# A chunked recurrence followed by an MLP on one Trainium2 core: preparing each chunk on 120 full rows with products in column tiles, one masking eviction, no early weights, and another scheduling mode

## The chip, the core and the metric

The kernel runs on one NeuronCore of a Trainium2 chip. Its engines are TensorE (PE, whose weight loads stand apart as PEld), VectorE (DVE), ScalarE (ACT), GpSimd (POOL) and SyncE (SP); DMAs are issued from queues of SP and POOL. The metric is the device time of one execution in microseconds (us), and smaller is better.

## What is computed

For 32 heads (4 batches x 8) a state of 40x40 is carried over 768 steps. Each step reads the state and then changes it; afterwards all heads of a token, 320 numbers, go through two dense layers.

```python
for t in range(S):
    y[:, :, t] = np.einsum('bhd,bhde->bhe', rt, state)
    Sa = np.einsum('bhde,bhe->bhd', state, at)
    state_decay = state * wt[:, :, None, :] - np.einsum('bhd,bhe->bhde', Sa, bt)
    state = state_decay + np.einsum('bhd,bhe->bhde', vt, kt)
...
h = x @ w_in
sp = np.where(h > 20.0, h, np.log1p(np.exp(np.minimum(h, 20.0))))
g = h * np.tanh(sp)
return (g @ w_out).astype(np.float32)
```

`x` is 3072 x 320, `w_in` 320 x 2048, `w_out` 2048 x 320. All inputs are 64-bit; the recurrence's inputs are turned to 32-bit on the host, and the weights are turned to 32-bit pairs (a high and a low part) on the chip.

## The kernel before

The 768 steps are cut into 12 chunks of 64, each taken with matrix products. Four kinds of work make up a chunk, and chunks are taken in pairs.

**Preparation** (`pre_a`, L126 to L203), twice per chunk, once for each half `be` of the heads. It loads the decays and `a` (tile `wa`) and `b`, `k` (tile `bk`) into rows 0 to 39 and 64 to 103, two heads groups `al` of 40 rows, so 80 of 128 rows carry data. On DVE it forms running products of the decays with two scans (L147, L157), scales `a` (L152) and `b`, `k` (L170). ACT copies the scaled `a` into a block layout `ad` (L155), one half on rows 0 to 63 and the other below, so that one PE product per slot (L186, 128 rows by 128 columns by 168 moving columns) gives all inner products of the two heads in that slot; the zeros of the layout keep the heads apart. There are 8 slots per call, and three groups of up to three slots are taken out of PSUM: two scaled copies into `GP` (L188, L189) and one copy into `HA` (L190) on ACT, a masked product into `HA` (L191) on DVE, and one more mask over `GP` (L193). PE transposes `bk` (L202), ACT takes that out (L203). The products of the decays, `P`, go to memory from POOL's queue (L172) for the second part of the kernel. The tiles `wa`, `bk`, `ad` and `P` have two buffers each; the tiles in PSUM named `pa` have two here.

**Inverse** (`pre_inv`, L205 to L221) once per pair of chunks: one transposition on DVE (L209), 60 small DVE operations one after another (L214, L216), and two transpositions (L218, L220). `post_inv` (L223 to L260) makes of it the tiles `KT` with PE products (L232, L241, L258) and ACT copies.

**Step** (`step_a` to `step_c`, L273 to L346) once per chunk, in two halves `g` of the heads: it carries the state from chunk to chunk: products L284, L293, L304, L314, L334, L339 on PE, evictions on ACT, masks (L316) and the state's update (L342, L346) on DVE. Its inputs are loaded from POOL's queue (L267, L270, L271), and `yD` is stored from it (L370).

**MLP** (L482 to L612): weights arrive in pieces (`split`, L488; `load_f32`, L446): a DMA into `cv_d` (L453), then one ACT operation (L459), three on DVE (L461 to L463), one on ACT (L494) and one on DVE (L495). One buffer serves all pieces. 12 pieces make `w_in`, 8 make `w_out`. `early` (three pieces of `w_in`) has its own memory from the start; `first` (the other nine) uses the memory that the preparation's pools leave, so it follows the last preparation; `second` starts `w_out`. Then `load_x` reads `yD` and `pD` back, and per block of 512 tokens PE makes 8 rounds of the first product (L584) and the second (L604 to L606).

The order on each engine is set by the tile framework's scheduler, from priorities: the tables `OFF`, `SORD` and `ORDER` move pieces of the program up or down. The first four chunks are prepared ahead of the first step; each later pair is prepared two pairs ahead.

Of the kernel before, what the change touches and what calls it, by code (L numbers as in the profile page):

```python
# [7 lines left out]
F32 = mybir.dt.float32  # L8
# [5 lines left out]
C = 64  # L14

NHA = 8
NBKN = 8
NA = 2
NWA = 2
# [5 lines left out]
NGP = 2  # L25
# [5 lines left out]
NAD = 2  # L31
NTMP = 1
NP = 2
# [14 lines left out]
def layouts(inp, S=768):  # L48
# [30 lines left out]
def attention(ctx, tc, I, yD, pD, nch, M):  # L79
# [28 lines left out]
    for w, b in zip(wab, bkb):  # L108
        V.memset(w, 1.0)
        G.memset(b, 0.0)  # L110
    for t in [d1] + [x.rearrange("p s k a t -> p (s k a t)") for x in adb[:NAD]]:
        A.copy(t, z.broadcast_to(t.shape))
# [10 lines left out]
    RW, W2, HA, BKN, GP, KT = {}, {}, {}, {}, {}, {}  # L123
    LQ, SQ, OQ, PQ = (dict(S=SP, G=G, A=A)[x] for x in QS)

    def pre_a(c, be):  # L126
        n = 2 * c + be
        wa, bk, ad = wab[n % NWA], bkb[n % NWA], adb[n % 2]
        for al in range(2):
            q = slice(al * 64, al * 64 + 40)  # L130
            LQ.dma_start(out=wa[q], in_=I['wa'][c, be, al])
        for al in range(2):
            q = slice(al * 64, al * 64 + 40)
            LQ.dma_start(out=bk[q, :, 0:128], in_=I['bk'][c, be, al])
        if (c, be) == (0, 0):
            LQ.dma_start(out=cst, in_=I['cst'])
            for t in bkb:
                A.copy(t[:, :, 128:168], cst[:, 256:296].unsqueeze(1).broadcast_to([128, 8, 40]))
        wz, a = wa[:, 0:521], wa[:, 528:1040]
        P = pw.tile([128, 520], F32, name="P", bufs=NP)  # L140
        E = wa[:, 520:1040]
        w2 = pw.tile([128, 2, 8], F32, name="w2", bufs=4)
        wz3 = wz[:, 0:520].rearrange("p (s j) -> p s j", j=65)

        V.tensor_reduce(out=w2[:, 0], in_=wz3[:, :, 1:33], axis=AX.X, op=ALU.mult)
        V.reciprocal(d1[:, 64:584:65], w2[:, 0])
        V.tensor_tensor_scan(out=P, data0=wz[:, 0:520], data1=d1[:, 64:584], initial=0.0, op0=ALU.mult, op1=ALU.add)  # L147
        P3 = P.rearrange("p (s j) -> p s j", j=65)
        E3 = E.rearrange("p (s j) -> p s j", j=65)
        V.tensor_copy(w2[:, 1], P[:, 64:520:65])  # L150
        a3 = a.rearrange("p (s t) -> p s t", t=64)
        V.tensor_tensor(out=a3, in0=a3, in1=P3[:, :, 0:64], op=ALU.mult)  # L152
        for al in range(2):
            q = slice(al * 64, al * 64 + 64)
            A.copy(ad[q, :, :, al], a[q].rearrange("p (s k t) -> p s k t", k=2, t=32))  # L155
        V.reciprocal(d1[:, 64:584:65], w2[:, 1])
        V.tensor_tensor_scan(out=E[:, 0:519][:, ::-1], data0=wz[:, 2:521][:, ::-1], data1=d1[:, 1:520][:, ::-1],  # L157
                             initial=0.0, op0=ALU.mult, op1=ALU.add)
        W2[be] = w2
        if be == 1:  # L160

            RW[c] = wk.tile([128, 2, 16], F32, name="rw", bufs=4)
            pt = ps_g.tile([128, 2, 16], F32, name="pa")
            for b2 in range(2):
                for al in range(2):
                    PE.matmul(pt[b2 * 64:b2 * 64 + 64, al], ident[:, al * 64:al * 64 + 64], W2[b2].rearrange("p a b -> p (a b)"),
                              start=(al == 0), stop=True, skip_group_check=True)
            A.copy(RW[c], pt)
        bk4 = bk[:, :, 0:128].rearrange("p s (x t) -> p s x t", x=2)
        V.tensor_tensor(out=bk4, in0=bk4, in1=E3[:, :, 0:64].unsqueeze(2).broadcast_to([128, 8, 2, 64]), op=ALU.mult)  # L170
        for al in range(2):
            PQ.dma_start(out=pD[c, be, :, al], in_=P[al * 64:al * 64 + 40])  # L172

        if c % 2 == 0 and be == 0:
            GP[c // 2] = iw.tile([128, 32, 2, 32], F32, name="GP", bufs=NGP)
        gp = GP[c // 2]
        u0 = (c % 2) * 16 + be * 8
        ha = iw.tile([128, 8, 104], F32, name="HA", bufs=NHA)
        HA[c, be] = ha
        oa, oh = (0, 40) if be == 0 else (64, 0)  # L180
        og, ok = (0, 64) if be == 0 else (64, 0)
        for s0 in (0, 3, 6):
            m = min(3, 8 - s0)
            pt = ps_g.tile([128, 3, 168], F32, name="pa")
            for j in range(m):
                PE.matmul(pt[:, j], ad[:, s0 + j].rearrange("p k a t -> p (k a t)"), bk[:, s0 + j], start=(j == 0), stop=True,  # L186
                          skip_group_check=True)
            A.mul(gp[0:64, u0 + s0:u0 + s0 + m, 1], pt[0:64, 0:m, og:og + 32], -1.0)  # L188
            A.mul(gp[64:128, u0 + s0:u0 + s0 + m].rearrange("p u k i -> p u (k i)"), pt[64:128, 0:m, og:og + 64], -1.0)  # L189
            A.copy(ha[:, s0:s0 + m, oa:oa + 40], pt[:, 0:m, 128:168])  # L190
            V.tensor_tensor(out=ha[:, s0:s0 + m, oh:oh + 64], in0=pt[:, 0:m, ok:ok + 64],  # L191
                            in1=maskH.unsqueeze(1).broadcast_to([128, m, 64]), op=ALU.mult)
        V.tensor_tensor(out=gp[:, u0:u0 + 8, 1], in0=gp[:, u0:u0 + 8, 1], in1=maskG.unsqueeze(1).broadcast_to([128, 8, 32]),  # L193
                        op=ALU.mult)

        bkn = wk.tile([128, 664], F32, name="bkn", bufs=NBKN)
        BKN[c, be] = bkn
        G.memset(bkn[:, 640:664], 0.0)
        for s0 in (0, 4):
            pt = ps_g.tile([128, 4, 2, 64], F32, name="pa")  # L200
            for j in range(4):
                PE.transpose(pt[:, j].rearrange("p a b -> p (a b)"), bk[:, s0 + j, 0:128], ident)  # L202
            A.copy(bkn[:, s0 * 80:s0 * 80 + 320].rearrange("p (s a e) -> p s a e", a=2, e=40), pt[:, :, :, 0:40])  # L203
# [61 lines left out]
    def step_loads(c):  # L265
        for be in range(2):
            SQ.dma_start(out=VS[be][vrow[be], :, 0:320], in_=I['vN'][c, be].rearrange("i (g s) d -> i g (s d)", g=2))  # L267
# [391 lines left out]
```

## Time and profile before

| what | us |
|---|---|
| three timed runs | 823.36, 827.55, 829.61 (median 827.55) |
| span of the profiled execution | 821.8 |
| PE busy | 722.7 (88% of the span) |
| DVE busy | 458.7 (56%) |
| ACT busy | 428.7 (52%) |
| first inverse ends on DVE (end of L220) | 100.5 |
| sixth inverse starts on DVE (L209) | 368.3 |
| first product of the MLP on PE (L584) | 460.7 |

The times are of whole executions; the span runs from the first to the last instruction of one profiled execution, and no time of its own is given beside it, so it is read against the runs: it is 1.6 under the fastest of them and 5.8 under their median. Four stages are told apart by the events of the last three rows: the start, the steady part, the transition and the MLP.

### The profile page before, as it was taken

The page shows a single profiled execution, that of the slowest core. Times are in us where ns is not written, and L with a number is a line of the kernel's source. Part 1 is how long each engine was busy: PE and PEld are TensorE (multiplying, and loading weights), DVE is VectorE, ACT ScalarE, POOL GpSimd, SP SyncE. Part 2 cuts the span into 40 slices and gives each one's busy share as a digit, 9 for nine tenths or more (in the row PEclk, how much of TensorE's full clock was granted, in tenths as well). Part 3 has the DMA queues.
Part 4 walks back from the last instruction along what each step waited for, and adds up shares of the span by engine and source line. Part 5 has one row for each costly group of instructions (what it writes and reads, how often), then busy time and mean ns, then how long its engine had stood idle before and what let it go on. Part 6 is the DMA issues. An engine that isn't in the chain of part 4 may idle for free.

```text
span 821.8 us, 17217 instructions
## 1 busy us (share of the span) xinstructions
PE 722.7 (88%) x7048; PEld 644.8 (78%) x7048; DVE 458.7 (56%) x957; ACT 428.7 (52%) x931; POOL 103.4 (13%) x182
## 2 busy tenths in 40 slices
PE   2635798899889889888786899999999999999997
PEld 2524697788778778788676789999999999999997
DVE  6689878749899757988954558311312212111110
ACT  5533556784586867567685555343333333432331
POOL 8100012123223022221102100000000000000000
PEclk9855679999999999999999999999999999999999
DMA  6522224323433134423528755210300100000000
GB/s 169 143 65 81 57 53 96 99 67 97 118 103 76 59 96 105 83 58 111 142 76 207 160 157 135 59 51 1 77 33 0 55 17 1 33 1 1 33 1 32
DMA packets 58206, 61.81 MB, mean 75 GB/s; under 512 B 25536, under 2 KB 48704, under 8 KB 58128
## 3 DMA queue, kind: packets, MB, share of 16 engines
q1 hardware_dynamic: 49296, 40.94, 18.3%
q0 software_dynamic: 8832, 19.79, 10.0%
q8 instruction: 55, 0.90, 0.5%
q14 instruction: 23, 0.19, 0.1%
HBM read 48.79 MB, written 11.86 MB: 74 GB/s over the span
## 4 chain that ended last, share of the span: by engine, by line
PE 52%; ACT 9%; DVE 7%; DMA 3%; issue 2%; SPq 0%; ACTq 0%; DVEq 0%
PE ph L584 21%; PE po L605 7%; PE po L604 7%; PE po L606 7%; PE pa L258 2%; PE pa L186 2%; DMA xp<-pD 1%; DVE tmp L214 1%; DVE XL L216 1%; PE pq L314 1%; ACT bdT L249 1%; PE pu L284 1%; ACT bdT L250 1%; DMA cv_d<-in_wi 1%; ACT KT L260 1%
## 5 line engine op out<-in xcount | busy, mean ns | idle before, releaser
L590 DVE TENSOR_TENSOR gl<-g,gh 128x1024 fp32r<-128x1024 f32 x48 | 58.6, 1224 | 207.5 <-ACT gh L589 207.5
L586 ACT ACTIVATE g<-ph 128x512 f32<-128x512 f32 x96 | 57.3, 598 | 180.5 <-PE ph L584 180.3
L186 PE MATMUL pa<-bk,ad 128*128 128x168 f32 x384 | 85.6, 376 | 42.8 <-DVE bk L170 15.0
L604 PE MATMUL po<-w_oh,gh 128*128 128x320 f32 x384 | 118.3, 308 | 0.0
L605 PE MATMUL po<-w_ol,gh 128*128 128x320 f32 x384 | 118.3, 308 | 0.0
L606 PE MATMUL po<-w_oh,gl 128*128 128x320 f32 x384 | 118.3, 308 | 0.0
L584 PE MATMUL ph<-xh,w_ih 128*128 128x512 f32 x288 | 112.7, 393 | 2.0 <-ACT xh L568 2.0
L186 PEld LDWEIGHTS pa<-bk,ad 128*128 128x128 f32 x384 | 71.5, 235 | 48.2 <-issue 22.8
L584 PE MATMUL ph<-xh,w_il 128*128 128x512 f32 x288 | 97.1, 391 | 0.0
L584 PE MATMUL ph<-xl,w_ih 128*128 128x512 f32 x192 | 75.1, 391 | 0.0
L605 PEld LDWEIGHTS po<-w_ol,gh 128*128 128x128 f32 x384 | 72.1, 188 | 2.2
L604 PEld LDWEIGHTS po<-w_oh,gh 128*128 128x128 f32 x384 | 72.1, 188 | 1.8
L606 PEld LDWEIGHTS po<-w_oh,gl 128*128 128x128 f32 x384 | 72.1, 188 | 0.0
L584 PEld LDWEIGHTS ph<-xh,w_ih 128*128 128x128 f32 x288 | 54.1, 188 | 12.1 <-ACT xh L568 2.2
L584 PEld LDWEIGHTS ph<-xh,w_il 128*128 128x128 f32 x288 | 54.0, 188 | 11.6 <-issue 0.2
L216 DVE TENSOR_TENSOR XL<-XL,tmp 128x30 f32<-128x30 f32 (+9 forms) x180 | 58.7, 326 | 2.4
L214 DVE TENSOR_TENSOR tmp<-XL 128x30 f32<-128x30 f32 (+9 forms) x180 | 58.2, 324 | 2.3
L258 PE MATMUL pa<-bdT,HA 128*104 128x128 f32 x384 | 52.2, 289 | 7.0 <-ACT bdT L251 5.5
L258 PEld LDWEIGHTS pa<-bdT,HA 128*104 128x104 f32 x384 | 46.7, 179 | 11.1 <-ACT bdT L251 7.2
L314 PE MATMUL pq<-bdr,UVT 128*128 128x128 f32 x384 | 53.4, 284 | 0.4 <-ACT UVT L286 0.3
L334 PE MATMUL pq<-UVQ,bkn 128*64 128x104 f32 (+1 forms) x768 | 44.7, 254 | 7.8 <-DVE UVQ L316 5.5
L589 ACT CAST gh<-g 128x1024 fp32r<-128x1024 f32 x48 | 50.1, 1048 | 1.3
(89 smaller groups left out, 1212.6 us busy)
## 6 DMA issues: line engine op xcount, KB each, us to landing
wa<-in_wa SPq DMA_DIRECT2D x48, 162.5 KB
bk<-in_bk SPq DMA_DIRECT2D x48, 160.0 KB
cv_d<-in_wi SPq DMA_DIRECT2D x12, 512.0 KB
cv_d<-in_wo SPq DMA_DIRECT2D x8, 640.0 KB
pD<-P POOLq DMA_DIRECT2D x48, 81.2 KB, 2.2
VS<-in_vN POOLq DMA_DIRECT2D x24, 160.0 KB, 3.4
UVT<-in_vD POOLq DMA_DIRECT2D x24, 160.0 KB, 3.9
bdr<-in_rD POOLq DMA_DIRECT2D x24, 160.0 KB, 4.4
```

Source lines behind the costliest of these rows:

```text
L186: PE.matmul(pt[:, j], ad[:, s0 + j].rearrange("p k a t -> p (k a t)"), bk[:, s0 + j], start=(j == 0), stop=True, skip_group_check=True)
L214: V.tensor_tensor(out=tv, in0=X[:, i + 1:32, i:i + 1].broadcast_to([128, 31 - i, i]), in1=X[:, i:i + 1, 0:i].broadcast_to([128, 31 - i, i] ...
L216: V.tensor_tensor(out=X[:, i + 1:32, 0:i], in0=X[:, i + 1:32, 0:i], in1=tv, op=ALU.add)
L258: PE.matmul(pk[:, j], ha[:, s0 + j], bd[:, s0 + j].rearrange("p a t -> p (a t)"), start=(j == 0), stop=True, skip_group_check=True)
L314: PE.matmul(pq[:, s], UVT[:, g * 4 + s, be * 128:be * 128 + 128], br[:, be, g * 4 + s].rearrange("p a t -> p (a t)"), start=(s == 0), stop ...
L584: PE.matmul(ph, w, x, start=(n == 0), stop=(n == 7), skip_group_check=True)
L586: A.activation(g[:, j], ph, AF.Mish)
L589: A.copy(gh, g)
L590: V.tensor_tensor(out=gl, in0=g, in1=gh.bitcast(F32), op=ALU.subtract)
L604: PE.matmul(po[k], gh[:, j, t], oh, start=(f == 0), stop=False, skip_group_check=True)
L605: PE.matmul(po[k], gh[:, j, t], ol, start=False, stop=False, skip_group_check=True)
L606: PE.matmul(po[k], gl[:, j, t], oh, start=False, stop=(f == 15), skip_group_check=True)
```

## The change

`pre_a` is called once per chunk. The host packs the eight groups of 40 rows into three blocks of 40, so 120 rows carry data, with 12 slots of 64 columns (four of the last block are empty). One DMA fills `wa` and one `bk`; `wa` and `P` now have one buffer, `bk` and `ad` two. Since the three blocks of a slot belong to different heads, `ad` holds the scaled `a` three times, each multiplied by a mask of one block of rows (L158). A slot of the earlier kernel (two heads) now takes six PE products of 120 rows by 32 columns (L192), with 64, 64, 168, 168, 104 and 104 moving columns, which go to column groups 0, 1, 2, 3, 0, 1 of 32 columns each. A group of three slots leaves PSUM in one DVE product with a mask that holds signs too (L194), into one tile `GA` that stands for `GP` and `HA`. Transposes are 12 instead of 16 per chunk (L203). `VS`, `UVT`, `yD` and `pD` have other layouts; three DMAs per chunk store `pD` instead of four, and four load `UVT` instead of two. No weights have memory of their own from the start (`NQ0 = 0`). The tile context is made with `schedule_with_timeline_sim=True`, so the order on all engines is set anew. Lines after the change are one to eight higher than before.

```diff
-NHA = 8
-NBKN = 8
+NBKN = 4
-NWA = 2
+NWA = 1
+NBK = 2
-NGP = 2
+NGA = 2
-NP = 2
+NP = 1
...
+    def dense(x):
+        x = x.transpose(4, 2, 1, 3, 6, 0, 5).reshape(nch, 8, 40, 4, C)
+        x = np.concatenate([x, np.zeros_like(x[:, :1])], 1)
+        return np.ascontiguousarray(x.reshape(nch, 3, 3, 40, 4, C).transpose(0, 1, 3, 2, 4, 5)).reshape(nch, 120, 12, C)
...
+    def place(be, s, al):
+        m = be * 4 + al * 2 + s // 4
+        return m % 3 * 4 + s % 4, m // 3
...
+        LQ.dma_start(out=wa[D], in_=I['wa'][c])
+        LQ.dma_start(out=bk[D], in_=I['bk'][c])
...
-        for al in range(2):
-            q = slice(al * 64, al * 64 + 64)
-            A.copy(ad[q, :, :, al], a[q].rearrange("p (s k t) -> p s k t", k=2, t=32))
+        for h in range(3):
+            m = 12 if h < 2 else 8
+            A.mul(ad[D, 0:m, h], a3[:, 0:m], mask3[D, h:h + 1])
...
-                PE.matmul(pt[:, j], ad[:, s0 + j].rearrange("p k a t -> p (k a t)"), bk[:, s0 + j], start=(j == 0), stop=True,
-                          skip_group_check=True)
-            A.mul(gp[0:64, u0 + s0:u0 + s0 + m, 1], pt[0:64, 0:m, og:og + 32], -1.0)
-            A.mul(gp[64:128, u0 + s0:u0 + s0 + m].rearrange("p u k i -> p u (k i)"), pt[64:128, 0:m, og:og + 64], -1.0)
-            A.copy(ha[:, s0:s0 + m, oa:oa + 40], pt[:, 0:m, 128:168])
-            V.tensor_tensor(out=ha[:, s0:s0 + m, oh:oh + 64], in0=pt[:, 0:m, ok:ok + 64],
-                            in1=maskH.unsqueeze(1).broadcast_to([128, m, 64]), op=ALU.mult)
-        V.tensor_tensor(out=gp[:, u0:u0 + 8, 1], in0=gp[:, u0:u0 + 8, 1], in1=maskG.unsqueeze(1).broadcast_to([128, 8, 32]),
-                        op=ALU.mult)
+                    for i in range(3):
+                        for al in range(2):
+                            slot, h = place(be, s0 + j, al)
+                            k = int(i == 1)
+                            o, q = slice(k * 64 + al * 32, k * 64 + al * 32 + 32), slice((0, 0, 64)[i], (64, 168, 168)[i])
+                            x = bk[D, slot, 0:32].unsqueeze(1).broadcast_to([120, 2, 32]) if i == 0 else bk[D, slot, q]
+                            PE.matmul(pt[o, j, q], ad[D, slot, h, k * 32:k * 32 + 32], x, start=(j == 0 and i < 2), stop=True,
+                                      skip_group_check=True)
+                V.tensor_tensor(out=ga[:, u0 + s0:u0 + s0 + m], in0=pt[:, 0:m], in1=maskA.unsqueeze(1).broadcast_to([128, m, 168]),
+                                op=ALU.mult)
...
-NQ0 = 1
+NQ0 = 0
...
-    with tile.TileContext(nc) as tc:
+    with tile.TileContext(nc, schedule_with_timeline_sim=True) as tc:
```

The new mode and the missing memory move nearly every row; three places matter below.

SP's queue at the last preparation's loads, before (`cv_d` is the buffer of weight pieces, `in_wi` is `w_in`, `in_wo` is `w_out`):

```order
L131 DMA wa_97<-in_wa 40x1040 x2
L134 DMA bk_98<-in_bk 40x8x128 x2
L134 DMA bk_99<-in_bk 40x8x128 x2
L453 DMA cv_d<-in_wi 128x1024 x9
L453 DMA cv_d<-in_wo 128x1280
L472 DMA xy<-yD 128x256
```

and now:

```order
L138 DMA wa_90<-in_wa 120x1560
L139 DMA bk_92<-in_bk 120x2016
L454 DMA cv_d<-in_wi 128x1024 x10
L454 DMA cv_d<-in_wo 128x1280
L473 DMA xy<-yD 128x256
```

Nine pieces of `w_in` stood behind the last load and ahead of the first read of `yD`; now it is ten, and of the two that are loaded at the start the second cannot be converted before the first one's results have memory.

PE at the end of the last preparation (L186 or L192 are its products, L202 or L203 its transposes, which release its memory), before:

```order
L186 MATMUL pa<-bk_99,ad_101 128x168 x2
L232 MATMUL pa<-TT,GP 32x32 x19
L202 MATMUL pa<-cst,bk_99 128x128 x8
L241 MATMUL pa<-X_4209,GP 32x32 x32
L258 MATMUL pa<-bdT_103,HA 104x128 x8
```

and now:

```order
L340 MATMUL pq<-bdr_108,smd 64x2x64
L258 MATMUL pa<-bdT_96,GA 104x128 x8
L340 MATMUL pq<-bdr_108,smd 64x2x64 x3
L203 MATMUL pa<-cst,bk_92 128x120 x4
L283 MATMUL pu<-KT,VS_103 64x64 x8
```

The last eight transposes stood together; now four of them stand with the last products L192, four among L242, and these last four some thirty rows later, behind half a step's products (L335, L340) and part of `post_inv`.

DVE where a later chunk is prepared among the steps (order prints a scan as SCALAR_TENSOR_TENSOR; L342 or L343 and L346 or L347 are the state's update), before:

```order
L342 TENSOR_TENSOR stn<-ST_122,pq 128x160
L147 SCALAR_TENSOR_TENSOR P<-wa_97,d_102 128x520
L346 TENSOR_TENSOR ST_122<-stn,R 128x8x40
L150 COPY w_2082<-P 128x8
L152 TENSOR_TENSOR wa_97<-wa_97,P 128x512
```

and now, in the eighth chunk:

```order
L343 TENSOR_TENSOR stn<-ST_109,pq 128x160
L194 TENSOR_TENSOR GA<-pa,cst 128x336
L150 SCALAR_TENSOR_TENSOR P<-wa_90,d_95 120x780
L347 TENSOR_TENSOR ST_109<-stn,R 128x8x40
L194 TENSOR_TENSOR GA<-pa,cst 128x504
```

The scan L150 writes the one buffer `P`, so it waits until the store of the chunk before is done; behind it on DVE stands the state's update L347. On POOL that store stands behind the loads of a step (L174 is the store, L269 and L270 are the step's loads):

```order
L269 DMA UVT<-in_vD 40x8x64 x2
L174 DMA pD<-P 40x3x260 x2
L174 DMA pD<-P 40x2x260
L269 DMA UVT<-in_vD 40x8x64 x2
L199 MEMSET bkn 128x24
L270 DMA bdr_108<-in_rD 40x16x64 x2
```

Before, each scan had a second buffer of `P`, so it waited for the store of the call before the last.

More of the change, by code (lines that the diff above doesn't have):

```diff
@@ L107, in attention @@
     V.memset(z, 0.0)
[L108 to L112, printed above, removed]
+    A.copy(d1, z.broadcast_to(d1.shape))
     for t in bdT:
@@ L121, in attention @@
         G.memset(t, 0.0)
-    RW, W2, HA, BKN, GP, KT = {}, {}, {}, {}, {}, {}
+    RW, BKN, GA, KT = {}, {}, {}, {}
     LQ, SQ, OQ, PQ = (dict(S=SP, G=G, A=A)[x] for x in QS)
-    def pre_a(c, be):
-        n = 2 * c + be
-        wa, bk, ad = wab[n % NWA], bkb[n % NWA], adb[n % 2]
-        for al in range(2):
[L130 to L135, printed above, removed]
-            LQ.dma_start(out=cst, in_=I['cst'])
[L137 to L143, printed above, removed]
+    D = slice(0, 120)
@@ L159, in pre_a @@
[L159 to L180, printed above, removed]
@@ new lines, in pre_a @@
+        V.reciprocal(d1[D, 64:844:65], w2[:, 1])
+        V.tensor_tensor_scan(out=E[:, 0:779][:, ::-1], data0=wz[:, 2:781][:, ::-1], data1=d1[D, 1:780][:, ::-1],
+                             initial=0.0, op0=ALU.mult, op1=ALU.add)
+        RW[c] = wk.tile([128, 2, 2, 8], F32, name="rw", bufs=4)
+        pt = ps_g.tile([128, 2, 16], F32, name="pa")
+        for be in range(2):
+            for h, l, n in (((0, 0, 3), (1, 0, 1)), ((1, 1, 2), (2, 0, 2)))[be]:
+                c0 = (h * 3 + l - be * 4) * 4
+                PE.matmul(pt[be * 64:be * 64 + 64, :, c0:c0 + 4 * n], sel3[:, h], w2[:, :, l * 4:l * 4 + 4 * n],
+                          start=(c0 == 0), stop=True, skip_group_check=True)
@@ L223, in post_inv @@
     def post_inv(n, TT, T1):
-        gp = GP[n]
+        ga = GA[n]
         for h in range(2):
@@ L333, in step_c @@
                     for be in range(2):
-                        PE.matmul(py[be * 64:be * 64 + 64, 2 * j + al, 0:n], BKN[c, be][:, u * 40:u * 40 + 64], UVQ[be][:, u, 0:n],
+                        slot, h = place(be, g * 4 + s, al)
+                        o = (slot * 3 + h) * 40
+                        PE.matmul(py[be * 64:be * 64 + 64, 2 * j + al, 0:n], BKN[c][:, o:o + 64], UVQ[be][:, u, 0:n],
                                   start=(j == 0 and al == 0), stop=(c == 0), skip_group_check=True)
@@ L376, in pa @@
             for c in range(2):
-                for be in range(2):
-                    with at(tc, 'p%d' % n), at(tc, 'P%d%d' % (c, be) if n else ''):
-                        pre_a(2 * n + c, be)
+                with at(tc, 'p%d' % n), at(tc, 'P%d0' % c if n else ''):
+                    pre_a(2 * n + c)
     def inv(n):
@@ L388, in attention @@
     inv(0)
-    for u in range(4):
-        with at(tc, 'P%d%d' % (u // 2, u % 2)):
-            pre_a(2 + u // 2, u % 2)
+    for u in range(2):
+        with at(tc, 'P%d0' % u):
+            pre_a(2 + u)
     for n in range(nds):
```

129 lines of the change are left out of this document (73 added, 56 removed).

## The prediction

> **What bounds the kernel now.** First I cut the span at three events: the end of the first inverse on DVE (100.5), the start of the sixth (368.3), and the first product of the MLP (460.7). The view of windows gives busy time in each:
>
> ```profile
> core 0: us, PE busy (x) PEld busy (x) DVE busy (x) ACT busy (x) POOL busy (x), PEclk, DMA share, GB/s
> 0.00:100.50 100.50, 51.68 (x270) 43.57 (x272) 81.38 (x184) 45.70 (x124) 24.61 (x46) 0.74 0.39 105
> 100.50:368.30 267.80, 240.40 (x3439) 213.25 (x3434) 214.51 (x540) 182.10 (x478) 60.00 (x108) 0.97 0.34 85
> 368.30:460.70 92.40, 74.44 (x1266) 65.25 (x1265) 65.08 (x145) 64.12 (x137) 15.89 (x24) 0.98 0.51 131
> 460.70:821.80 361.10, 356.21 (x2084) 322.73 (x2084) 97.78 (x93) 136.82 (x195) 2.90 (x5) 0.99 0.17 45
> ```
>
> At the start DVE is the busy engine (81.4 of 100.5) and PE runs at a granted clock of 0.74. In the steady part PE is busy 90%, DVE 80%, ACT 68%: PE is nearest to its limit, and DVE, whose inverse is one long chain, is second. In the last stage PE is never free.
>
> The third stage has no full engine, so I read the chain of waits and the timeline there:
>
> ```profile
> 369.14 0.37 SPq L453 DMA_DIRECT2D cv_d<-in_wi  x1
> 434.70 0.33 SPq L453 DMA_DIRECT2D cv_d<-in_wo  x1
> 437.95 0.33 SPq L472 DMA_DIRECT2D xy<-yD  x1
> ```
>
> ```profile
> 384.59 4.25 DMA cv_d<-in_wi
> ...
> 451.24 5.87 DMA xp<-pD
> 457.33 1.77 DVE xy L567
> 459.12 1.48 ACT xh L568
> 460.65 1.56 PE ph L584 x4
> ...
> 792.00 3.65 PE ph L584 x16
> ...
> 799.18 3.65 PE ph L584 x16
> ```
>
> Nine pieces of weights go through one buffer, from 369.14 to 434.70: 65.6/9 = 7.3 us each, 4.25 of it the DMA. Only behind them does the queue read `yD`, and the MLP starts 22.7 later. The first piece starts 0.9 after the sixth inverse does, when the last preparation lets go of its memory. So the transition is a chain that hangs on the **last preparation**, not on the steps. The MLP then takes 7.18 per round (799.18 - 792.00), 48 rounds, 344.6.
>
> **The change, stage by stage.** *Steady part, on PE.* The rows of this stage (lines view, same window):
>
> ```profile
> L186 PE MATMUL pa<-bk,ad 128*128 128x168 f32 x256 | 48.7, 328 | 1.4 <-DVE HA L191 1.2
> L314 PE MATMUL pq<-bdr,UVT 128*128 128x128 f32 x256 | 36.8, 287 | 0.1
> L258 PE MATMUL pa<-bdT,HA 128*104 128x128 f32 x256 | 34.5, 288 | 3.3 <-ACT bdT L251 2.1 <-ACT KT L260 1.0
> L334 PE MATMUL pq<-UVQ,bkn 128*64 128x104 f32 x512 | 29.8, 256 | 3.9 <-DVE UVQ L316 2.3 <-ACT yev L343 1.5
> L284 PE MATMUL pu<-KT,VS 104*64 104x64 f32 x512 | 26.6, 229 | 0.9 <-ACT smd L305 0.6 <-ACT KT L260 0.2
> L202 PE MATMUL pa<-cst,bk 128*128 128x128 f32 x126 | 21.9, 288 | 4.6 <-ACT bkn L203 2.5 <-DVE HA L191 1.6
> L293 PE MATMUL pu<-cst,UVT 128*128 128x128 f32 x128 | 18.1, 279 | 3.2 <-ACT UVT L286 3.1
> L339 PE MATMUL pq<-bdr,smd 128*64 128x128 f32 x224 | 17.4, 273 | 0.0
> ...
> L304 PE MATMUL pu<-cst,ST 128*128 128x128 f32 x56 | 9.0, 283 | 2.3 <-ACT UVQ L294 2.2
> ```
>
> A product of 32-bit numbers is two records, a transpose one. L186 had 128 products here, eight chunks' worth, at 0.38 each. In the new order six chunks stand ahead of the first inverse's end, so six are left: 96 slots. What a slot costs, now six products on 32 columns each, no row shows. What column tiles do is seen in L284, two groups of 64 columns on the same rows:
>
> ```profile
> 271.07 1.15 PE L284 MATMUL pu<-KT,VS 104*64 104x64 f32 x32
> ```
>
> ```profile
> 247.41 0.69 PE L284 MATMUL pu<-KT,VS 104*64 104x64 f32 x16 [0.17 <-ACT KT L260]
> ```
>
> ```profile
> 247.41 0.28 PE L284 MATMUL pu<-KT,VS 104*64 104x64 f32 x2 [0.17 <-ACT KT L260]
> ```
>
> Eight products more take 1.15 - 0.69 = 0.46, 0.0575 each for 64 moving columns. The third row is a look at 0.05 us alone: two records have begun, so two groups work at once. A slot has 64 + 64 + 168 + 168 + 104 + 104 = 672 columns. Two at a time: 672 x 0.0575/64 = 0.60 (one at a time, 1.2). Four at a time, 168 columns go through each group, as many as through the whole array in a slot of L186, so 0.38 stays. Between 0.38 and 0.60 (+0.05 for changeovers, the difference of L186 here to its 0.33 in a run of twelve records) I take 0.41, near the lower end, because the groups of L284 and of the 32-column products L232 run beside each other without any visible order, and column loads are even (168 on all four groups).
>
> ```profile
> 276.97 1.98 PE L186 MATMUL pa<-bk,ad 128*128 128x168 f32 x12
> ```
>
> The Trainium skill, in "TensorE: Matmul & The Clock Gate" (Part 3, measured speedup), gives 2.38 for three column tiles; by that a slot would be 1.2/2.38 = 0.50, an estimate, and the sum 9 higher.
>
> PE: 240.4 - 48.7 - 21.9 + 96 x 0.41 + 72 transposes x 0.174 = 221.7; and since in the new order half a step less stands ahead of the sixth inverse, a sixteenth of the six step rows (137.7) goes too, 8.6: 213. Of the 27.4 idle some 3 (half of what L186 and L202 waited for evictions) goes and perhaps 2 by the order: 22 are left. **235 instead of 267.8.**
>
> *DVE and ACT in it.* One eviction takes the place of four:
>
> ```profile
> L147 DVE TENSOR_TENSOR_SCAN P<-wa,d 128x520 f32<-128x520 f32 x24 | 29.6, 1233 | 0.2
> ...
> L170 DVE TENSOR_TENSOR bk<-bk,wa 128x1024 f32<-128x1024 f32 x24 | 29.1, 1213 | 0.4 <-DMA bk<-in_bk 0.2
> ...
> L316 DVE TENSOR_TENSOR UVQ<-pq,cst 128x512 f32<-128x512 f32 x48 | 32.9, 685 | 14.5 <-PE pq L314 14.3
> ...
> L155 ACT COPY ad<-wa 64x512 f32<-64x512 f32 x48 | 29.6, 617 | 13.7 <-DVE wa L152 7.9 <-issue 3.8 <-PE pa L186 0.6
> ...
> L191 DVE TENSOR_TENSOR HA<-pa,cst 128x192 f32<-128x192 f32 x48 | 17.0, 355 | 26.3 <-ACT HA L190 24.2 <-PE pa L186 2.0
> L152 DVE TENSOR_TENSOR wa<-wa,P 128x512 f32<-128x512 f32 x24 | 16.4, 684 | 0.0
> ...
> L193 DVE TENSOR_TENSOR GP<-GP,cst 128x256 f32<-128x256 f32 x24 | 9.9, 414 | 1.8 <-ACT GP L189 1.8
> ```
>
> DVE's old chunk is two calls: scans 4 x 1.23, L170 2 x 1.21, L152 2 x 0.68, L191 and its mask about 2 x 1.4, small ones 2 x 0.97: 13.5. The new one: scans 2 x 1.85, L171 1.74 (the slope of L152 to L170 is 1.03 per 1000 elements), L155 0.95, six evictions of 504 or 336 elements at L316's rate 3.7, small ones 1.1: 11.2. The evictions cost more than those removed (2.8), 75% of the scans' columns pays for it. ACT drops its three per group; its three copies of `ad` are 2 x 0.85 and 0.62. DVE idled 24.2 for `HA`; that wait goes. DVE's share of the stage stays below PE's (about 186 of 235), so it gives no term of its own.
>
> *The start.* Scans of nine calls stood ahead of the inverse's end (4.5 chunks); now six chunks' do, with four chunks' evictions, because `schedule_with_timeline_sim` put them there. The inverse's sixty operations in this stage:
>
> ```profile
> L216 DVE TENSOR_TENSOR XL<-XL,tmp 128x30 f32<-128x30 f32 (+14 forms) x30 | 9.8, 327 | 0.2
> ...
> L214 DVE TENSOR_TENSOR tmp<-XL 128x30 f32<-128x30 f32 (+14 forms) x30 | 9.6, 319 | 0.3
> ```
>
> With its transpositions it is 24.7. Sum: 6 x 7.5 + 4 x 3.7 + 24.7 + a weight piece 1.8 = 86, and as neighbours overlap (rows of this stage sum to 92.6 for 81.4 busy) 76. Idle comes on top: `wa` has one buffer, so each load of 731 KB starts when L171 is done. From 4.25 (as for a piece of 512 KB) to 6.1 (in proportion); I take 6: 6 for the first, 6 for the second, about 3 uncovered for each of four more, and 1 to 1.5 per chunk where L160 waits for ACT's three copies: 31. **107 instead of 100.5.**
>
> *The transition.* It has one DMA piece more (7.3), the second piece's conversion that no longer hides at the start (3.5), and the last four transposes behind half a step's products (24 of L335, 11 of L340, 8 of L258 at 0.12, 0.16, 0.27: 6.7, of which 5.5): 92.4 + 16.3 = **109**; bounds 103 (no delay by transposes) and 113 (all, and the first conversion waits its turn on DVE).
>
> *The MLP.* 344.6, a tail of 5.8, and of the old remaining 10.7 of the last step half, because only L335 and L340 stand behind the first product: **355.5**.
>
> Sum: 107 + 235 + 109 + 355.5 = 806.5, 15.3 under 821.8. That span is 5.8 under the median of the runs; I take the difference off the median: 827.55 - 15.3 = **812**.
>
> **Rivals.**
>
> A, *the whole relief arrives*: PE's idle time falls to 9 (its waits were for evictions and for ACT) and pieces run without the transposes' delay: stage two 222, stage three 103: 787.5, **793**. For it: ACT loses over half of its work in a preparation. Against: half of PE's idle rows (L258, L293, L304) wait for ACT work that stays.
>
> B, *the transition eats it*: idle on PE stays 27.4 and 3 more, start 110, chain 113: 820.5, **826**. For it: the chain of weights is longer by construction, and nothing in the steps shortens it.
>
> C, *column products go two at a time*: the second record of a product waits on its own columns and holds back the products behind it. From 0.60 + 0.05 per slot on it decides: 96 x 0.24 = 23 in the steady part, 5 at the start at the clock of 0.74: 834.5, **840**. For it: only two groups at once are ever seen. Against: the even load of four groups.
>
> D, *one buffer of P*: a scan waits for a store that stands on POOL's queue behind the step's loads; the state's update waits behind it on DVE.
>
> ```profile
> pD<-P POOLq DMA_DIRECT2D x48, 81.2 KB, 2.2
> ...
> UVT<-in_vD POOLq DMA_DIRECT2D x24, 160.0 KB, 3.9
> ```
>
> Two issues and a landing are about 5 in five chunks (7 to 11): 25 if none is covered: 831.5, **837**.
>
> E, *weight loads stand alone*: each of the 12 loads of a slot is exposed.
>
> ```profile
> L232 PEld LDWEIGHTS pa<-TT,GP 32*32 32x32 f32 x768 | 15.4, 110 | 7.1 <-DVE TT L218 2.3 <-ACT KT L260 2.2 <-issue 1.7
> ```
>
> 96 x 12 x 0.11 = 127 more: **939**. The Trainium skill says so in the same Part 3 ("What overlaps and what doesn't"): a weight load overlaps a running matmul only if the row groups differ, and here they do not. The trace disagrees for two groups: 16 products' records of L284, all on the same rows, took 0.69 with their loads.
>
> **How the numbers follow.** Forecast 0.40 (own range 803 to 821), A 0.18, B 0.21, C 0.12, D 0.07, E 0.02. The range 793 to 840 leaves out some 0.1 on either side. About 1% (8 us) can be told from no change in this kernel. Faster by over 1% (below 819): most of the forecast, A, a little of B: 0.55. Within 1%: 0.26. Slower (above 836): C, E, most of D and a bit of B: 0.19.
>
> **What would show it.** First inverse's end at 107 (95 to 113). L192 in a run of 18 products: 1.0 to 1.3 is right, 1.8 is C, over 4 is E. PE share of the steady part above 90%. The sixth inverse at 342. `cv_d` at 7.3 per piece, ten of them, and the MLP's first product 109 behind the sixth inverse; if it comes within 100, A; if DVE's scans show waits for `pD` of 5 each, D. Wrong would be a steady part of 260 or more with L192 at its forecast price, or an MLP that starts when the steps end and not when the weights do.

## The result, and where the time went

The changed kernel takes 900.99 us (median; 895.79 to 903.45), the kernel before 825.99 beside it: ratio 1.0897, interval 1.085 to 1.0944. The profiled execution of the change took 895.79 us with a span of 894.0; before it was 821.8. The view of windows, cut at the same three events (end of the first inverse, start of the sixth, first product of the MLP):

```profile
core 0: us, PE busy (x) PEld busy (x) DVE busy (x) ACT busy (x) POOL busy (x), PEclk, DMA share, GB/s
0.00:117.35 117.35, 51.27 (x974) 44.22 (x976) 79.23 (x143) 25.90 (x42) 25.41 (x42) 0.77 0.56 132
117.35:422.31 304.96, 276.02 (x4551) 226.25 (x4546) 197.03 (x443) 141.21 (x311) 65.15 (x99) 0.93 0.31 72
422.31:540.23 117.92, 96.83 (x1392) 86.62 (x1391) 75.01 (x160) 69.80 (x146) 26.14 (x37) 0.84 0.49 119
540.23:894.02 353.79, 348.90 (x2019) 316.48 (x2017) 95.62 (x91) 132.64 (x189) 1.29 (x2) 1.00 0.16 44
```

| stage | before | forecast | after |
|---|---|---|---|
| start | 100.5 | 107 | 117.4 |
| steady part | 267.8 | 235 | 305.0 |
| transition | 92.4 | 109 | 117.9 |
| MLP | 361.1 | 355.5 | 353.8 |

The steady part holds most of the miss: 70 us against the forecast. PE's idle time in it (305.0 - 276.0 = 29) hardly differs from before (27.4); its *busy* time grew by 36, although its work should have shrunk. ACT fell from 182 to 141 and DVE from 215 to 197, as the change intends (over the whole span ACT falls from 428.7 to 369.6 and DVE from 458.7 to 446.9). The rows of PE in this stage:

```profile
L192 PE MATMUL pa<-bk,ad 120*32 120x104 f32 (+2 forms) x1464 | 78.1, 272 | 10.4 <-DVE GA L194 9.3 <-issue 1.0
L313 PE MATMUL pq<-bdr,UVT 128*128 128x128 f32 x253 | 38.3, 301 | 9.0 <-DMA bdr<-in_rD 7.7 <-issue 1.3
L283 PE MATMUL pu<-KT,VS 104*64 104x64 f32 x512 | 31.2, 232 | 0.1
```

L192 has 1464/12 = 122 slots, 0.64 us each, while L186 had 128 at 0.38. To see why, the timeline of PE is read at two places: where products of L192 stand one behind the other, and where the order sets them between others.

```profile
186.97 1.06 PE L192 MATMUL pa<-bk,ad 120*32 120x64 f32 x36 [1.47 <-DVE GA L194]
189.64 0.78 PE L192 MATMUL pa<-bk,ad 120*32 120x64 f32 x24 [1.04 <-DVE GA L194]
...
250.89 0.47 PE L192 MATMUL pa<-bk,ad 120*32 120x168 f32 x2
251.30 0.24 PE L233 MATMUL pa<-TT,GA 32*32 32x32 f32 x2
251.47 0.47 PE L192 MATMUL pa<-bk,ad 120*32 120x168 f32 x2
251.87 0.24 PE L233 MATMUL pa<-TT,GA 32*32 32x32 f32 x2
252.04 0.37 PE L192 MATMUL pa<-bk,ad 120*32 120x104 f32 x2
252.34 0.24 PE L233 MATMUL pa<-TT,GA 32*32 32x32 f32 x2
```

18 products in a row (36 records, three slots) take 1.06, so 0.35 a slot, and this is within what was forecast (1.0 to 1.3 for such a run). Alone, one product of 168 columns takes 0.41 until the next may start (250.89 to 251.30), one of 104 columns 0.30. With 0.23 for 64 columns, a slot of such loners would be near 1.9. Over the whole stage, from one start to the next: 1262 records in runs of nine or more took 41.4 us (33 ns each), and 164 records in pairs between other lines took 25.5 (156 ns each). So 82 lone products of 732 cost as much as some 385 in runs.

DVE also waits where it did not wait before. The view of waits, DVE, at the start and in the steady part:

```profile
DVE w L148 <- DMA wa<-in_wa: 23.2, 6, 6.0
DVE wa L160 <- ACT ad L158: 5.3, 2, 4.1
DVE cv_w L462 <- ACT cv_m L460: 4.0, 1, 4.0
...
DVE bk L171 <- DMA bk<-in_bk: 22.3, 6, 5.9
...
DVE w L148 <- DMA wa<-in_wa: 9.3, 4, 4.6
```

In the kernel before, DVE waited 0.2 us for `bk` in these two stages and not at all for `wa`. These waits reach the end of the kernel. The page of the profile follows the chain of work that ended last; its shares of the span are, before and then after:

```profile
PE 52%; ACT 9%; DVE 7%; DMA 3%; issue 2%; SPq 0%; ACTq 0%; DVEq 0%
```

```profile
PE 63%; DMA 16%; DVE 13%; ACT 5%; issue 2%; POOL 0%; SPq 0%; DVEq 0%; ACTq 0%
```

Of the 16% for DMAs, 6 are loads of `wa` and 3 loads of `bk`. The row of L313 above shows one more load: PE itself waited 7.7 us for `bdr` in the steady part, where it did not before. No run here takes that wait apart.

The windows also show PE's granted clock. It was 0.97 in the steady part and 0.98 in the transition before, and is 0.93 and 0.84 now. A lower clock makes the same products last longer, in this trace a run of 18 (1.06 above) 1.91 where the clock was 0.50:

```profile
352.34 1.91 PE L192 MATMUL pa<-bk,ad 120*32 120x64 f32 x36
```

SP's queue shows the transition:

```profile
362.02 0.33 SPq L139 DMA_DIRECT2D bk<-in_bk  x1
436.56 71.61 SPq L454 DMA_DIRECT2D cv_d<-in_wi  x10
511.31 0.33 SPq L454 DMA_DIRECT2D cv_d<-in_wo  x1
516.54 0.33 SPq L473 DMA_DIRECT2D xy<-yD  x1
```

Ten late pieces at (511.31 - 436.56)/10 = 7.5 us. The first starts 14.3 behind the sixth inverse (422.31), where it was 0.9 before.

### The profile page after: what moved, and what is told of

Its sections match the earlier page's. It is cut to its first block, busy times and chain, and to the rows that moved or that the text cites. A ratio compares the mean times of both kernels' runs of the same rounds, so it can differ in the third digit from the quotient of the medians.

```text
span 894.0 us, 20375 instructions
## 1 busy us (share of the span) xinstructions
PE 773.0 (86%) x8920; PEld 673.6 (75%) x8920; DVE 446.9 (50%) x835; ACT 369.6 (41%) x687; POOL 118.0 (13%) x180
## 4 chain that ended last, share of the span: by engine, by line
PE 63%; DMA 16%; DVE 13%; ACT 5%; issue 2%; POOL 0%; SPq 0%; DVEq 0%; ACTq 0%
PE ph L585 20%; PE po L607 6%; PE po L606 6%; PE po L605 6%; DMA wa<-in_wa 6%; PE pa L192 5%; PE pq L313 4%; PE pa L258 3%; PE pq L335 3%; DMA bk<-in_bk 3%; DMA cv_d<-in_wi 3%; DMA bdr<-in_rD 2%; PE pu L283 2%; DVE P L150 2%; DVE bk L171 2%
## 5 line engine op out<-in xcount | busy, mean ns | idle before, releaser
L192 PE MATMUL pa<-bk,ad 120*32 120x104 f32 (+2 forms) x2304 | 116.6, 307 | 39.0 <-DVE GA L194 27.4
L192 PEld LDWEIGHTS pa<-bk,ad 120*32 120x32 f32 x2304 | 79.7, 130 | 54.4 <-DVE GA L194 31.5
L585 PE MATMUL ph<-xh,w_ih 128*128 128x512 f32 x288 | 112.4, 392 | 0.0
L313 PE MATMUL pq<-bdr,UVT 128*128 128x128 f32 x384 | 62.8, 323 | 14.1 <-DMA bdr<-in_rD 12.1
L313 PEld LDWEIGHTS pq<-bdr,UVT 128*128 128x128 f32 x384 | 57.1, 232 | 16.7 <-issue 14.9
L158 ACT ACTIVATE ad<-wa,cst 120x768 f32<-120x768 f32 (+1 forms) x36 | 29.0, 856 | 79.3 <-DVE wa L155 63.9
L194 DVE TENSOR_TENSOR GA<-pa,cst 128x504 f32<-128x504 f32 (+1 forms) x72 | 43.2, 609 | 33.2 <-PE pa L192 33.1
L258 PE MATMUL pa<-bdT,GA 128*104 128x128 f32 x384 | 53.8, 293 | 2.2 <-ACT KT L260 1.3
```

The source lines that it names most:

```text
L192: PE.matmul(pt[o, j, q], ad[D, slot, h, k * 32:k * 32 + 32], x, start=(j == 0 and i < 2), stop=True, skip_group_check=True)
L194: V.tensor_tensor(out=ga[:, u0 + s0:u0 + s0 + m], in0=pt[:, 0:m], in1=maskA.unsqueeze(1).broadcast_to([128, m, 168]), op=ALU.mult)
L258: PE.matmul(pk[:, j], ga[:, us.start + s0 + j, 64:168], bd[:, s0 + j].rearrange("p a t -> p (a t)"), start=(j == 0), stop=True, skip_group ...
L313: PE.matmul(pq[:, s], UVT[:, g * 4 + s, be * 128:be * 128 + 128], br[:, be, g * 4 + s].rearrange("p a t -> p (a t)"), start=(s == 0), stop ...
L585: PE.matmul(ph, w, x, start=(n == 0), stop=(n == 7), skip_group_check=True)
```

## The experiments

Three theories to begin with. Theory 1: products on 32 columns are cheap only behind each other, and the new order takes them apart. Theory 2: the loads of `wa` and `bk` are late. Theory 3: the timeline scheduler's order as a whole is the loss. After four runs theory 4 joined them: the weights that are no longer loaded early. The times, and the stages of each profiled execution (us; e9 and e14, which ran once, stand further down). The stages belong to one execution, whose time lies under the median by 5 in the change, by 7 in e3 and e10 and by 4 in e5, and 4 above it in e12, so small differences between stages of different runs say little:

| run | time | ratio to before, interval | start | steady | transition | MLP |
|---|---|---|---|---|---|---|
| e1_no_timeline | 880.84 | 1.0614 (1.056 to 1.0668) | 104.0 | 291.9 | 131.8 | 351.2 |
| e2_before_timeline | 885.41 | 1.0655 (1.0587 to 1.0722) | 122.7 | 292.4 | 106.9 | 362.0 |
| e3_two_wa | 887.65 | 1.0684 (1.0611 to 1.0758) | 112.4 | 278.0 | 132.2 | 356.2 |
| e4_runs_whole | 875.3 | 1.0556 (1.0496 to 1.0617) | 116.6 | 278.6 | 124.2 | 352.3 |
| e5_before_late_weights | 847.45 | 1.0227 (1.0163 to 1.0291) | 106.6 | 271.9 | 107.4 | 355.6 |
| e6_old_order_two_wa | 860.62 | 1.0389 (1.0324 to 1.0454) | 100.8 | 266.1 | 140.6 | 352.4 |
| e7_transposes_first | 852.53 | 1.0297 (1.0223 to 1.0372) | 102.0 | 280.3 | 116.3 | 351.9 |
| e8_transposes_first_timeline | 863.66 | 1.0418 (1.0347 to 1.0489) | 117.6 | 275.9 | 116.4 | 351.7 |
| e10_early_weights_back | 843.12 | 1.0222 (1.0142 to 1.0301) | 108.6 | 266.2 | 98.8 | 361.1 |
| e11_before_two_early | 894.75 | 1.0856 (1.0773 to 1.094) | 99.4 | 336.5 | 96.5 | 359.1 |
| e12_early_weights_one_bk | 851.68 | 1.0333 (1.0257 to 1.041) | 105.2 | 292.5 | 97.0 | 359.5 |
| e13_change_early_weights | 868.61 | 1.0458 (1.0403 to 1.0513) | 112.4 | 287.6 | 105.7 | 362.8 |

**Whole runs (e4).**

```diff
-PE.matmul(pt[o, j, q], ...)
+with tc.high_priority(offset=j * 6 + i * 2 + al):
+    PE.matmul(pt[o, j, q], ...)
```

> The changed kernel, where all products of one group of L192 carry the priority of the group's first, so that the scheduler issues them in one run: 3 products of L192 stand alone instead of 82, 5 of L283's instead of 39, 19 of L233's instead of 38. Nothing else is changed. Theory 1: L192 in the steady part falls from 78 us busy to 49 and the rest of the rows by 10 or more: the steady part is 35 to 45 shorter, 855 to 866. Theory 2: the loads wait as before: 888 to 902. Theory 3: as the order is otherwise the mode's own, 885 to 902.

Measured: 875.3, 26 less than the change (lines of this kernel are one higher from here on).

```profile
116.61:395.17 278.56, 238.17 (x4585) 207.74 (x4581) 193.05 (x437) 142.79 (x317) 62.43 (x95) 0.94 0.32 77
```

PE's busy time in the steady part falls from 276.0 to 238.2, by 37.8, about as theory 1 priced it. The row of the products alone gives 27 of it (78.1 before):

```profile
L193 PE MATMUL pa<-bk,ad 120*32 120x168 f32 (+2 forms) x1464 | 50.8, 273 | 12.6 <-DVE GA L195 8.7 <-ACT bkn L205 2.7 <-issue 1.0
```

The stage does not hold quite the same work in both runs, but over the whole span PE's busy time falls by more, from 773.0 to 730.0. The time falls by less, because PE's idle time in the steady part grows from 29 to 40; at 875.3 it lies outside theory 1's 855 to 866, and outside the 885 and more of the others. DVE's waits in that part:

```profile
DVE bk L171 <- DMA bk<-in_bk: 25.5, 6, 6.1
DVE w L148 <- DMA wa<-in_wa: 15.1, 5, 4.4
```

They are 9 longer than in the change (40.6 for 31.6), so it seems that the loads stood behind the lone products. Theory 1 is shown, as a part of the loss and not all of it.

**The scheduler's mode, off and on (e1, e2).**

```diff
-with tile.TileContext(nc, schedule_with_timeline_sim=True) as tc:
+with tile.TileContext(nc) as tc:
```

> The changed kernel without the timeline scheduler, nothing else undone. Theory 1, alternation: a slot of L192 costs 0.40 us in a run of its own (33 ns per record in runs of nine or more) and 156 ns per record where the order sets one of its products between products of other shapes; L283 and L233 lose in the same way, some 45 us of the steady part. In this order 41 products of L192 stand alone instead of 82, so half of it goes: 875 to 885, and L192 still shows singles at 150 ns or more. Theory 2, one buffer of wa: the loads' waits (wa and bk on the chain, 9% of the span) stay: 890 to 905. Theory 3, the scheduler's order as a whole is the loss, whatever the alternation does: 820 to 845.

> The kernel before, with the timeline scheduler alone. Theory 1: its 128-column products cannot overlap and lose nothing to alternation, and fewer of the small products stand alone than in the order before (17 to 12 for L284): 820 to 835. Theory 2: its two buffers of wa stay: 820 to 835. Theory 3: the mode's order delays preparation and steps here too: 850 to 880.

Measured: off in the change, 880.84, 20 less (theory 1 had said 875 to 885), with lone products at 156 ns still (82 records for 164), and DVE's waits for `wa` and `bk` in the first two stages at 29.6 for 54.8; both moved, so this run does not part them. On in the kernel before, 885.41, 58 more than before, and that kernel has no column products in L186. Theories 1 and 2 had said 820 to 835, theory 3 850 to 880. The waits of DVE in e2, start and steady part:

```profile
DVE w L145 <- DMA wa<-in_wa: 17.1, 9, 3.7
...
DVE w L145 <- DMA wa<-in_wa: 19.5, 8, 3.8
DVE bk L170 <- DMA bk<-in_bk: 18.5, 9, 4.0
```

With two buffers per operand, as before, DVE now waits 55 us for loads. The mode sets the reads of `wa` and `bk` ahead of the moment at which they land on the chip. This is a cost of the order, whatever is prepared. It is not the only one: PE has the same products and is busy 740.0 us instead of 722.7, at a granted clock of 0.89 in the steady part and 0.86 in the transition. How much of the 58 is the waits alone stays open. Theory 3 as "the whole loss" falls with e1 (820 to 845 expected), but the mode is a loss of its own.

**Two buffers of wa (e3).**

```diff
-NWA = 1
+NWA = 2
```

> The changed kernel with two buffers of wa (and of the E half in it); the timeline scheduler stays, so the order moves with it, 68 products of L192 alone instead of 82. Theory 1: only the start gains some 5 us and the alternation a fifth: 880 to 892. Theory 2: the waits for wa in the start (about 18 us in six) and in the steady part (9 us) go, and bk, which queues behind wa, comes earlier: 855 to 870. Theory 3: the order is what costs: 890 to 905.

Measured: 887.65, 13 less, inside theory 1's range (880 to 892) and outside theory 2's (855 to 870). The wait for `wa` in the steady part is gone, that for `bk` falls to 9.0. But of the 23.2 for `wa` in the start 20.2 stay, so a second buffer does not lift those; the start gains 5. The transition gives back 14: twelve pieces are late now instead of ten, and none is loaded at the start any more (the second buffer seems to take their room).

**Both together, in the old order (e6), then the transposes ahead (e7), then the mode again (e8).** e6 is e4's edit with `NWA = 2` and without the mode; e7 moves the block from `bkn = wk.tile(...)` to its last `A.copy` ahead of `if c % 2 == 0: GA[c // 2] = ...`; e8 is e7 with the mode.

> The changed kernel without the timeline scheduler, with two buffers of wa, and each group of L192 in one run. Theory 1 with theory 2 (alternation and loads are the whole loss in the steady part): against 881 without the timeline, 20 less by whole runs and 10 to 15 less by the loads: 846 to 856, steady part 255 to 262. Rival, the transition (132 there, 92 before) sets the end and takes it back: 868 to 880.

> The kernel of e6_old_order_two_wa with the block of transposes and bkn written ahead of the block of products and masking evictions. Theory 4: the late weights wait for the memory of the last preparation, which the last transposes hold (the first piece starts 14 to 31 us behind the sixth inverse where it was 0.9 before): the first piece then starts within 5 us of it, and the time falls by 15 to 25 against e6. Rival, the memory is held by something else or the steps set the end: within 6 us of e6, with the first piece more than 12 us behind.

> The kernel of e7_transposes_first with the timeline scheduler switched on again. Theory 2 in the form that the runs so far suggest (the mode's order puts DVE's reads of wa and bk where its model has the loads landed, and DVE waits there: 32 us in the steady part of the changed kernel, 38 in the kernel before with the mode, under 1 without it): 15 to 30 slower than e7, with such waits of 20 or more. Rival, the mode cost by alternation alone, which is gone here: within 6 of e7.

Measured: e6 860.62, between its two forecasts: steady part 266 as it was before, but a transition of 140.6. e7 852.53, 8 less. Its SP queue:

```profile
381.81 72.54 SPq L455 DMA_DIRECT2D cv_d<-in_wi  x10
...
481.41 0.33 SPq L474 DMA_DIRECT2D xy<-yD  x1
```

The first piece starts 0.5 *ahead of* the sixth inverse (382.32), in e6 26.5 behind it. So the last transposes do hold the memory of the late weights. The transition is 24 shorter, of which the steady part takes 14 back. It has as many transposes as in e6 (88) but more of the steps, with 512 records of L336 for 448, so the sixth inverse itself now stands later among the steps. The gain of 8 is below the 15 expected. e8, 863.66, is 11 slower than e7, all of it in the start (117.6 against 102.0). One row of DVE's waits in that stage carries this, first of e7, then of e8:

```profile
DVE w L148 <- DMA wa<-in_wa: 8.6, 2, 5.8
```

```profile
DVE w L148 <- DMA wa<-in_wa: 25.2, 4, 8.7
```

That is 16.6 more in a start that is 15.6 longer, with two buffers in both. No product of L192 (L202 in this kernel) but one stands alone in the steady part of e8's order, so this is the mode's cost without that alternation. It is below the 15 to 30 expected and above the 6 of the rival.

**Early weights (e5, e13, e10, e12, e11).** e5: the kernel before with `NQ0 = 0`. e13: the change with `NQ0 = 1, NAD = 1`. e10: e7 with `NQ0 = 1, NWA = 1, NAD = 1`. e12: e7 with `NQ0 = 1, NBK = 1, NAD = 1`. e11: the kernel before with `NQ0 = 2, NHA = 6`.

> The kernel before, with NQ0 = 0: no weight pieces at the start, all twelve late. Theory 4, the transition is a chain of weight pieces and the early ones shortened it: 7 to 18 more behind the sixth inverse, 2 to 5 less at the start, 833 to 842. Rival, the chain has slack since steps fill the time: 822 to 831.

> The changed kernel as it is, timeline scheduler and all, with NQ0 = 1 and one buffer of ad to make room; products of L192 alone 51 instead of 82. Theory 4, the early weights are worth 20 us by themselves: 870 to 882 against 901 (a part by the fewer singles). Rival, in the changed kernel the late pieces hide behind steps that are late anyway: 890 to 905.

> The kernel of e7_transposes_first with NQ0 = 1 (early weights as before), one buffer of wa and one of ad, which makes room for them. Theory 4: the early weights are worth the 20 us that they cost in the kernel before: 830 to 841, and the late chain has about three pieces less. Rival, single buffers of wa and ad take it back at the start and in the steady part: 848 to 862.

> The kernel of e7_transposes_first with NQ0 = 1, two buffers of wa, one of bk and one of ad. Theory 4: as e10, 830 to 841. Rival, a chunk's bk load now waits for the last product of the chunk before it, and DVE waits 5 or more per chunk for bk: 855 to 880.

> The kernel before with NQ0 = 2 (six of the twelve pieces early) and six instead of eight HA buffers, which makes room. Theory 4 at full strength, the transition ends with the weights whatever else is done: 805 to 818. Rival, with three pieces early the steps already end about when the weights do, and the start gets longer: 822 to 840.

Measured: without early weights the kernel before loses 21.6 us (e5, more than expected), with 15 more in the transition, 6 in the start and 4 in the steady part, and 6 less in the MLP. With them the changed kernel gains 32 (e13, 870 to 882 expected): the transition is 12 and the start 5 shorter, the MLP 9 longer; of the steady part's 17 some 8 are fewer lone products of L192 (102 records at 157 ns for 164). e10 comes to 843.12, its transition back at 98.8:

```profile
374.27 65.47 SPq L455 DMA_DIRECT2D cv_d<-in_wi  x9
449.73 0.33 SPq L455 DMA_DIRECT2D cv_d<-in_wo  x1
450.56 0.33 SPq L474 DMA_DIRECT2D xy<-yD  x1
```

Nine pieces, and the read of `yD` 76 behind the first (100 in e7). e10 gains 9 on e7, not the 12 to 22 expected: with one buffer of `wa` DVE waits 15.9 for it in the start (8.6 in e7) and 16.1 in the steady part (none in e7). e12 buys the room with `bk` instead and is 9 slower than e10, outside both of its ranges; the waits of 5 per chunk that its rival named are not there (3.3 in all). Its steady part holds more work than e10's (4952 records of PE for 4645), and over the whole span PE is busy 728.3 us for 714.2, at a granted clock of 0.90 in the steady part and 0.81 in the transition, where e10 has 0.95 in both. What lowers the clock is not explained here. e11, far above both of its ranges, says nothing on weights: its steady part grew by 69 us, with 48.8 of DVE's waits for `HA` copies on ACT (15.3 before), and the steps were late. More early weights were thus not tried in a fair way.

**What the columns do (e9, e14).** Each is e4 with the same products in another order, and each ran once.

```diff
-for j in range(m):
-    for i in range(3):
-        for al in range(2):
+for al in range(2):
+    for j, i in [(j, i) for k in range(2) for j in range(m) for i in ((0, 2), (1,))[k]]:
```

e14 has the same two loops with `al` inside.

> The kernel of e4_runs_whole with the products of each group of L192 in another order: first all that write one block of 32 output partitions, then the next block, so that neighbours share their column group; the products and their number are the same. Theory 1 as overlap of neighbours in different column groups: a slot's 672 columns go one after another, 1.2 us instead of 0.40 (about 100 ns per record, three times 33): 0.8 more for 122 slots in the steady part and 70 at the start, 975 to 1025. Rival, what costs is the switch from one shape or line to another, not the lost overlap: within 8 us of e4, 870 to 884.

> The kernel of e4_runs_whole with each group's products of L192 in the order of two column groups alternating (all of the first pair of blocks, then all of the second pair), the same products in number. If four groups do work at once in the order of the change (31 ns per record in a run), two give 45 to 63 ns per record (63 where one group follows itself), and the time goes up by 5 to 15 on e4: 880 to 890. If two at a time is all that the array does, the price stays at 31 to 34 ns: 870 to 880.

Measured: 896.44 and 874.52. The rows of 18 and of 12 products in e4, e14 and e9, from the timeline of PE:

```profile
202.23 1.06 PE L193 MATMUL pa<-bk,ad 120*32 120x64 f32 x36
...
174.93 0.78 PE L193 MATMUL pa<-bk,ad 120*32 120x64 f32 x24
```

```profile
302.09 1.67 PE L193 MATMUL pa<-bk,ad 120*32 120x64 f32 x36
303.86 1.09 PE L193 MATMUL pa<-bk,ad 120*32 120x64 f32 x24
```

```profile
361.64 2.58 PE L193 MATMUL pa<-bk,ad 120*32 120x64 f32 x36
...
263.90 1.41 PE L193 MATMUL pa<-bk,ad 120*32 120x64 f32 x24
```

Four groups 1.06, two groups 1.67, one group 2.58: neighbours in different column groups do work at once, and more than two of them. (Whether the products themselves or their weight loads lose the overlap with fewer groups was not parted.) In runs of nine or more this is 31, 42 and 63 ns per record in the steady part. e14's price, 42, lies between its two forecasts (45 to 63 and 31 to 34) and is well off the 31 of four groups. Its time lies in the range given for two groups being all that the array does (870 to 880), but also within e4's own spread (873.52 to 879.6), so the time does not decide; PE is busy 16 us more in the steady part (254.4 and 238.2). e9's time lies outside both of its ranges, 975 and more and 870 to 884: one group after another costs 0.75 a slot (63 ns x 12) and not 1.2, and 21 us in all. So the lost overlap explains 31 to 63 ns, and the 156 ns of a record that stands alone holds some 90 more. Its neighbours there are products of other shapes; what this second part is made of was not taken apart.

## Why the prediction was wrong, step by step

**The price of a slot was right in a run and was used where there is no run.** "I take 0.41": whole runs give 0.35 to 0.40 (x36 in 1.06, 33 ns per record). The row on which the choice leaned, two records of L284 begun within 0.05 us, cannot tell two groups from the two records of one product; that groups overlap is shown by e9 and e14. Rival C, two at a time, named 1.8 for this row and is out. So is E, with over 4. What failed is that one price was put on every slot. The prediction treated the scheduler as something that moves instructions ahead or back. It did not ask what stands next to them. 82 products of L192 stand alone in the new order, and L283 and L233 are taken apart too; this adds 38 us of PE's time (e4). No rival named it.

**"So six are left: 96 slots" was a wrong count.** Six chunks have *begun* on DVE before the first inverse ends, but PE has done 840/12 = 70 slots by then, and 122 are left (1464/12): 26 x 0.41 = 10.7 us. Of the half step that should have gone (8.6) only some 3 went: L335 has 482 records for 512 and L340 208 for 224, but L313 has 253 for 256, and L283, L292 and L303 have as many as before. With the 5 that stayed, 12 more transpose records (84 for 72: 2) and the 38, PE's 213 becomes 269; measured 276. The granted clock may hold the rest, 0.94 in e4's steady part and 0.97 before: as an estimate, 0.06 x 238 - 0.03 x 240 = 7. The prediction had no term for it. Idle time was taken as 22 and is 29.

**The gain forecast for the core of the change was not there.** e5 and e7 were timed side by side; neither has early weights or the mode, and both have two buffers of `wa` (in e5 of half a chunk each): 847.45 and 852.53. Over the whole span PE is busy 729.0 and 722.5, DVE 462.5 and 445.8, ACT 426.8 and 373.5. The relief lands on ACT and DVE. PE, which bounds the steady part, does about the same work: 0.37 a slot in e7 (47.6 us for 128), 0.38 in e5 (45.8 for 122). Whether an order tuned to the new preparation would show a gain was not tried. The prediction said itself that DVE's relief has no term, and then found its 33 us elsewhere: 9.3 in products (by the count of six chunks), 9.4 in transposes, 8.6 in the half step and 5.4 in idle time. (Its rows of DVE and ACT are those of the whole span; in the steady part DVE idled 15.3 for `HA`, not 24.2. And rival B's terms add up to 821.9, not 820.5. Neither changes the forecast.)

**The start was right in its waits for wa and short in the rest.** 24 of the 31 idle were for `wa`; measured 23.2. Beside 79.2 of DVE's work (forecast 76) stand 38 of idle time, with 4.0 for a weight piece's conversion and 2.3 for products that had no term. The end is 117.4, outside the 95 to 113 given.

**The transition's mechanism was right and its size short.** Pieces took 7.5 (7.3 forecast), ten of them. But the first one came 14.3 behind the sixth inverse, where 0.9 + 5.5 had been reckoned, and the way from the last piece to the first product is 28.9, 2.9 more than before. 117.9 instead of 109. Rival B had this mechanism with a chain of 113, too. e7 shows the cause that the prediction gave, the late transposes. That the early weights were worth 20 us to the kernel before was not seen: the prediction counted one piece and one conversion, 10.8.

**The MLP** came to 353.8 (355.5). **Rival D** found nothing: no wait of DVE for `pD` is in the change's lists of waits (e7 has one, of 2.8). **A** is out.

**What the prediction left out altogether** is the mode as a cost of its own. On the kernel before it costs 58 us (e2), on the corrected change 11 (e8), each time with DVE in front of loads that have not landed. The prediction had a term for one buffer of `wa`, and none for `bk`, whose waits are the larger ones in the steady part (22.3).

The last gap is not closed. e10, the best version of the change, stays 2.2% above before (1.4 to 3.0). With one buffer of `wa` for a whole chunk DVE waits 32 us for it there, 23 more than in e7. e12 has the second buffer of `wa` and the early weights, but only one of `bk`, and is slower; no kernel here has two of both and the early weights. The chain of work that ended last spends 4% of the span on loads of `wa` in e10, where e7's has 3% for `bk`; how much a second buffer would give back stays open.

## What to carry to other kernels

A product that uses a part of the array has two prices, in a run of its kind and alone: before one price is put on all of them, count in the new order how many stand alone. A new scheduling mode is a change by itself; try it alone on the old kernel, and look for engines that it parks in front of loads. What a change pays for its buffers (here the early weights) must be charged to it, and relief of engines that don't set the end is no income.

## What the runs showed of the hardware

Products of 32 output columns, 120 rows and 64 to 168 moving columns: 18 of them took 1.06 us with four column groups in turn, 1.67 with two and 2.58 with one, so four groups are worth 2.58/1.06 = 2.4. The Trainium skill, "TensorE: Matmul & The Clock Gate" (Part 3, measured speedup), gives 2.38 for three column tiles of 32 columns with 512 moving columns; the trace has about this much with four and 64 to 168. All of these products use the same rows, and their weight loads lie within the 1.06: the 36 of them, at 113 ns in the mean, overlap each other and the products and take 0.84 in all.

```profile
186.97 0.84 PEld L192 LDWEIGHTS pa<-bk,ad 120*32 120x32 f32 x36 [1.58 <-DVE GA L194]
```

A lone product may cost others, too. A full-width product of L313 (2 records) that stands between one of L233 and a lone one of L192 takes 0.42 from its start to the next (252.98 to 253.40), while in a run eight of its kind take 2.02, 0.25 each; the granted clock was 1.00 in both places. Here both neighbours have other shapes, so this price is not the lone product's alone.

```profile
133.40 2.02 PE L313 MATMUL pq<-bdr,UVT 128*128 128x128 f32 x16 [1.31 <-issue]
...
252.98 0.49 PE L313 MATMUL pq<-bdr,UVT 128*128 128x128 f32 x2
253.40 0.30 PE L192 MATMUL pa<-bk,ad 120*32 120x64 f32 x2
253.63 0.24 PE L233 MATMUL pa<-TT,GA 32*32 32x32 f32 x2
```
